# RWKV-6 attention followed by a token mixer: one exponential per unit, the last batch's values loaded like the rest, zero products in the array's gaps, and another order of steps

## Chip, core and metric

One core of a Trainium2 chip runs the whole kernel: one launch, inputs and output in device memory. The metric is the device time of one execution in microseconds (us). TensorE is called PE, VectorE DVE, ScalarE ACT, GpSimd POOL, and SyncE, which issues nearly all DMAs, SP.

## The reference

```python
for t in range(S):        # B, H, S, D = 4, 8, 768, 48
    cur = einsum('bhd,bhe->bhde', u * k[t], v[t])
    y[t] = einsum('bhd,bhde->bhe', r[t], state + cur)
    state = w[t][:, :, :, None] * state + einsum('bhd,bhe->bhde', k[t], v[t])
x = y.transpose(0, 2, 1, 3).reshape(B, S, H * D)          # 4 x 768 x 384
W = (x @ w_q) @ (x @ w_k).T / sqrt(64)                    # per batch
out = relu(W @ x) @ w_out
```

## The kernel before

A **unit** is 256 time steps of one batch, in two chunks (c = 0, 1) of 128; there are 12 units (n = 0 to 11), three to a batch. A partition holds two neighbouring steps (j = 0, 1) of each of the 8 heads, so a load (`load`, L231) moves 1024 pieces of 384 bytes for each of w, k, r and v. Per unit:

- `ln` (ACT, L409) takes the logarithm of w; `cw` (PE, L431) multiplies it with a triangular matrix CM, which gives cumulated sums in PSUM; `ep` and `en` (ACT, L447 and L455) take exp of plus and minus that. `ep` is two instructions, one for each j, because positions inside a chunk are laid out in four interleaved groups of 32 (the permutation matrix PM).
- `k16`, `r16`, `v16` cast to bf16; `kT`, `rT` (PE, L468) transpose k and r through PM; `ks` copies k out of PSUM; `qT` = r k; `RT` = r ep (DVE); `KT` = k en (POOL, or DVE).
- `vp` (PE, L549) brings v into the same order of positions, and `VB` copies it out of PSUM. For the last batch (`WHOLE`) there is no `v16` and no `vp`: four DMAs (`vw`, L244), one to each group of 32 partitions, bring the batch's values already in order, in pieces of 192 bytes, and `VB` casts from there.
- `A` (PE) = KT times RT per head and chunk; `AM` (DVE, L597) masks it, 24 times 1024 columns; `kb` and `kd` transpose and scale KT; `sn` and `SB` (PE, DVE L660) carry the state from chunk to chunk; `ya` and `yi` (PE) sum the output; `dps`, `dd`, `Vd` make the term of u; `X` (DVE, L712) adds both.
- `xt`, `XT`, `qk`, `QK` give the mixer's two projections. After a batch's last unit `T` and `TS` form one matrix for the batch, and per unit `mx`, `rl`, `fp`, `os`, `st` make the output: product, relu, product, copy, store.

The program is not written in this order. Each piece is a step, and three tables written out by hand set everything: `ORDER` (L82) is the order in which all steps are emitted, and so each engine's in-order queue, SP's of DMAs included; `WAYS` (L124) picks the engine of each step that can run on several; `BANKS` (L129) gives each PSUM buffer its bank. A step waits for its inputs and for the release of its buffer. Most buffers come in rings: four each for the loaded w, k, r, v and for the output (`os`), two for the rest. The steps `z` (L859) are fillers: one product of zeros with 512 columns into a PSUM bank, read by nobody; `WARM` = 12 of them stand in ORDER. Nine more such products open the program (L253).

Of the kernel before, what the change touches and what calls it, by code (L numbers as in the profile page):

```python
# [32 lines left out]
class Plan:  # L33
# [89 lines left out]
]  # L123
WAYS = (  # L124
    "PDDPDADDPDPAAPPAAccEADPPDdAAAPEDEcEAADPAdPAAPEDEEAAAAAAAAAAPDPPAAPEAcEEDDAPDdPDDPEAEEEDA"
    "PPDPPADPeAcEDAAAAAAAAPPAPPADPEAEcEAAPADPPADPEAEceDDPPDPPAAPeAceAAAADAADDPPDPPAPEAcEeAAPP"
    "DPPAPeAccEADPPDdPPAPPAEEADAEAAAADADAAAAAAADA"
)
BANKS = [  # L129
# [9 lines left out]
WARM = 12  # L139
# [3 lines left out]
def kernel(  # L143
# [14 lines left out]
    C = 128  # L158
# [12 lines left out]
    LONG = ()  # L171
    WHOLE = (B - 1,)
# [14 lines left out]
    def const(shape, dtype, name):  # L187
# [3 lines left out]
    EW = 136  # L191
# [5 lines left out]
        wg=(4, HW, F32), rg=(4, HW, F32), kg=(4, HW, F32), vg=(4, HW, F32), os=(4, 2 * DM, F32),  # L197
# [22 lines left out]
    PM = const([C, C], BF16, "PM")  # L220
# [15 lines left out]
    def load_long(b, i, tl, ap):  # L236
        for g in range(2):
            o = view(tl, 0, [[2 * D2, NP], [1, 2 * D2]], p0=g, pn=C - 1)
            o = dataclasses.replace(o, ap=[[2 * o.ap[0][0], 64]] + list(o.ap[1:]))
            nc.sync.dma_start(  # L240
                out=o,
                in_=ap[b, ds(g * NP, NP), ds(i * U, U)].rearrange("h (p s) d -> p h (s d)", s=4))

    def load_whole(b, q, tl):  # L244
        nc.sync.dma_start(
            out=view(tl, 0, [[D, H * NCH], [1, D]], p0=64 * (q % 2) + 32 * (q // 2), pn=32),
            in_=dataclasses.replace(v, offset=(b * H * S + q) * D,
                                    ap=[[4 * D, 32], [C * D, H * NCH], [1, D]]))

    def setup():  # L250
# [9 lines left out]
        for q in range(4):  # L260
            rows = ds(64 * (q % 2) + 32 * (q // 2), 32)
            nc.gpsimd.iota(pos0[rows, :], pattern=[[0, 1]], base=q, channel_multiplier=4)
            nc.gpsimd.iota(pos1[rows, :], pattern=[[0, 1]], base=q + 1, channel_multiplier=4)
# [3 lines left out]
        for c in range(2):  # L267
            for j in range(2):
                m = view(CM, j * C, [[64, 2], [32, 2], [1, 32]], p0=c * 64, pn=64)
                nc.gpsimd.affine_select(m, m, pattern=[[1, 2], [2, 2], [4, 32]],  # L270
                                        compare_op=ALU.is_ge, fill=0.0, base=-j,
                                        channel_multiplier=-2)
# [3 lines left out]
        nc.vector.memset(PM, 0.0)  # L276
        m = view(PM, 0, [[64, 2], [32, 2], [1, 32]])
        nc.gpsimd.affine_select(m, m, pattern=[[64, 2], [1, 2], [2, 32]],
                                compare_op=ALU.not_equal, fill=1.0, base=0,
                                channel_multiplier=-1)  # L280
# [5 lines left out]
        for q in range(4):  # L286
            m = view(US, 0, [[64, 2], [32, 2], [1, 32]], p0=64 * (q % 2) + 32 * (q // 2), pn=32)
            nc.gpsimd.affine_select(m, m, pattern=[[1, 2], [2, 2], [4, 32]],
                                    compare_op=ALU.is_gt, fill=0.0, base=-q,
                                    channel_multiplier=-4)  # L290
        for x in (tiles["lw"][1], tiles["k16"][1], tiles["r16"][1]):
            nc.vector.memset(view(x, D, pads), 0.0)
        nc.vector.tensor_scalar_mul(IDU, ID16, UNIT)
        nc.vector.tensor_scalar_mul(gk, gv, UNIT)
        nc.vector.tensor_scalar_mul(US, US, gv)

    def pads(e, x):
# [15 lines left out]
    def wide():  # L313
        return Buf("w")
# [581 lines left out]
```

## Time and profile before

| what | value |
|---|---|
| median of 3 runs | 104.68 us (104.49 to 104.9) |
| the profiled execution | 105.49 us, of which its span 103.8 us |
| instructions | 4460 |
| DMA | 24.68 MB in 56405 packets, mean 238 GB/s |
| loads | w, k, r: 12 each; v: 9, and vw: 4 |
| DVE, ACT, POOL steps | 125, 122, 55 |

The profile is of one execution. Its busy times count an engine from an instruction's start to its end, so neighbouring instructions of one engine overlap by some 0.07 us; where the cost in a row matters, the distance from start to start is used. Matmuls are pipelined with modelled ends, so a busy PE is not an array at its peak. PEclk is the clock granted to the array, 1.00 being the full one. A name such as AM(2,1) is the step AM of unit 2, chunk 1.

### The profile page before, as it was taken

How to read it: one execution, taken by the hardware profiler on the slowest of the kernel's cores; microseconds unless marked ns; L12 is line 12 of the kernel's file. 1: busy time of each engine (PE TensorE's matmuls, PEld its weight loads, DVE VectorE, ACT ScalarE, POOL GpSimd, SP SyncE). 2: the span in 40 equal slices, each digit the busy share in tenths (PEclk: the TensorE clock that was granted, in tenths of full speed). 3: DMA queues.
4: the chain of work that ended last, by engine and by line, in shares of the span. 5: the costliest groups of instructions: out<-in, count | busy, mean ns of one | idle time of the engine just before them, and what ended most of it. 6: DMA issues, size and time to landing. Idle time of an engine off the chain costs nothing.

```text
span 103.8 us, 4460 instructions
## 1 busy us (share of the span) xinstructions
PE 90.4 (87%) x1897; PEld 66.8 (64%) x1899; DVE 85.6 (82%) x155; ACT 81.4 (78%) x138; POOL 64.6 (62%) x78
## 2 busy tenths in 40 slices
PE   5997686999998999999998999979998999999800
PEld 2344564867876887677776877768677687867400
DVE  6295996897889999999999999999999899856020
ACT  6368787875899798899997999898988894938710
POOL 6808507576069979795798969989996456000000
PEclk9999995555579999999999999999999999999995
DMA  1999999989979999999999999998990087007691
GB/s 35 319 323 325 324 258 279 309 214 290 315 201 237 350 325 259 292 327 263 245 303 242 265 304 236 170 174 174 246 348 20 6 317 295 3 6 283 253 334 43
DMA packets 56405, 24.68 MB, mean 238 GB/s; under 512 B 54080, under 2 KB 55232, under 8 KB 56384
## 3 DMA queue, kind: packets, MB, share of 16 engines
q1 hardware_dynamic: 56224, 24.19, 84.9%
q8 instruction: 15, 0.25, 1.0%
q10 hardware_dynamic: 160, 0.20, 0.5%
q14 instruction: 6, 0.05, 0.1%
HBM read 19.66 MB, written 4.72 MB: 235 GB/s over the span
## 4 chain that ended last, share of the span: by engine, by line
PE 48%; DVE 17%; DMA 10%; ACT 9%; SPq 7%; issue 4%; DVEq 0%; ACTq 0%
PE PS L179 48%; SPq L232 7%; DMA wg<-in_w_dram 6%; DMA out_dram<-os 4%; DVE X L712 4%; DVE AM L597 3%; DVE qT L508 3%; DVE RT L518 2%; DVE ks L335 2%; ACT os L329 2%; ACT MX L341 2%; ACT lw L409 2%; ACT kd L331 1%; DVE SB L660 1%; ACT en L456 1%
## 5 line engine op out<-in xcount | busy, mean ns | idle before, releaser
L597 DVE TENSOR_TENSOR AM<-PS,US 128x1024 bf16<-128x1024 f32 x24 | 28.8, 1215 | 1.0 <-ACT lw L409 0.9
L528 POOL TENSOR_TENSOR KT<-ks,en 128x1024 bf16<-128x1024 bf16 (+1 forms) x9 | 17.2, 1914 | 12.1 <-PE PS L179 4.3
L577 POOL TENSOR_TENSOR Vd<-VB,dd 128x768 bf16<-128x768 bf16 (+1 forms) x14 | 18.4, 1317 | 3.2 <-ACT dd L329 1.9
L179 PEld LDWEIGHTS <-KT 48*128 48x128 bf16 (+1 forms) x300 | 10.8, 98 | 6.3 <-issue 4.0
L449 ACT ACTIVATE ep<-PS 128x512 bf16<-128x512 f32 (+1 forms) x28 | 13.6, 550 | 1.3 <-PE PS L179 1.2
L456 ACT ACTIVATE en<-PS 128x1024 bf16<-128x1024 f32 (+1 forms) x14 | 12.7, 912 | 2.2 <-PE PS L179 1.8
L179 PE MATMUL PS<-wo,MX 128*128 128x384 bf16 x72 | 13.4, 326 | 0.0
L712 DVE SCALAR_TENSOR_TENSOR X<-PS,gx,Vd 128x384 bf16<-128x384 f32 x22 | 12.5, 610 | 1.0 <-PE PS L179 0.7
L179 PE MATMUL PS<-RT,KT 48*128 48x128 bf16 x192 | 10.2, 228 | 1.7 <-POOL KT L528 0.4
L423 POOL CAST r<-rg 128x768 bf16<-128x768 f32 x10 | 8.4, 844 | 4.0 <-DMA rg<-in_r_dram 4.0
L409 ACT ACTIVATE lw<-wg 128x768 bf16<-128x768 f32 x12 | 10.2, 852 | 0.7 <-DMA wg<-in_w_dram 0.7
L331 ACT ACTIVATE kd<-PS,gk 128x768 bf16<-128x768 bf16 (+1 forms) x11 | 8.4, 762 | 1.4 <-PE PS L179 1.4
L341 ACT ACTIVATE MX<-PS 128x768 bf16<-128x768 f32 (+1 forms) x13 | 8.7, 688 | 0.7 <-PE PS L179 0.5
L179 PE MATMUL PS<-Z 128*128 128x512 bf16 x19 | 7.5, 522 | 1.8 <-DVE Z L252 1.2
L179 PEld LDWEIGHTS <-MX 128*128 128x128 bf16 x72 | 6.5, 98 | 3.9 <-issue 0.3
L518 DVE TENSOR_TENSOR RT<-PS,ep 128x1024 bf16<-128x1024 bf16 (+1 forms) x14 | 8.4, 605 | 0.8 <-ACT ep L449 0.8
L179 PE MATMUL PS<-VB,AM 128*128 128x48 bf16 x192 | 8.8, 189 | 0.0
L329 ACT COPY os<-PS 128x768 f32<-128x768 f32 (+1 forms) x11 | 7.3, 693 | 1.8 <-DMA out_dram<-os 1.0
L179 PE MATMUL PS<-CM,lw 64*128 64x128 bf16 x192 | 8.3, 232 | 0.4
L329 ACT COPY XT<-PS 128x768 bf16<-128x768 bf16 (+1 forms) x9 | 6.5, 732 | 2.5 <-PE PS L179 2.3
L508 DVE TENSOR_TENSOR qT<-PS,ks 128x1024 bf16<-128x1024 bf16 x12 | 8.2, 683 | 0.0
L179 PEld LDWEIGHTS <-lw 64*128 64x128 bf16 x192 | 6.3, 101 | 1.8 <-ACT lw L409 1.0
(90 smaller groups left out, 196.1 us busy)
## 6 DMA issues: line engine op xcount, KB each, us to landing
kg<-in_k_dram SPq DMA_DIRECT2D x12, 384.0 KB, 5.4
wg<-in_w_dram SPq DMA_DIRECT2D x12, 384.0 KB, 5.1
rg<-in_r_dram SPq DMA_DIRECT2D x12, 384.0 KB, 5.5
vg<-in_v_dram SPq DMA_DIRECT2D x9, 384.0 KB, 6.0
out_dram<-os SPq DMA_DIRECT2D x9, 384.0 KB, 4.1
vw<-in_v_dram SPq DMA_DIRECT2D x4, 288.0 KB, 6.6
out_dram<-os SPq DMA_DIRECT2D x5, 192.0 KB, 3.2
wof<-in_moe_w_out_dram SPq DMA_DIRECT2D x1, 576.0 KB, 6.4
```

The source lines that it names most:

```text
L179: return nc.tensor.matmul(o, l, rr, start=start, stop=stop, skip_group_check=True, is_transpose=trans)
L329: nc.scalar.copy(o, i)
L341: nc.scalar.activation(o, i, ACT.Relu)
L409: nc.scalar.activation(view(lw.tile, 0, [[64, H], [512, 2], [1, D]]), view(g["wg"].tile, 0, [[D2, H], [D, 2], [1, D]]), ACT.Ln, bias=0.0, ...
L449: nc.scalar.activation(view(ep.tile, cs[0] * NP * EW + off, [[EW, NP * len(cs)], [step, 2], [1, 32]]), view(at(cw), cs[0] * 512 + j * 64, ...
L456: nc.scalar.activation(en.tile[:, ds(cs[0] * 512, w_)], at(cw)[:, ds(cs[0] * 512, w_)], ACT.Exp, bias=0.0, scale=-1.0)
L508: lambda e: nc.vector.tensor_tensor(plain(qT.tile), turned(512), plain(ks.tile), ALU.mult),
L518: nc.vector.tensor_tensor(plain(RT.tile, cs, 32), turned(512, cs, True), plain(ep.tile, cs, EW // 4), ALU.mult)
L528: x.tensor_tensor(KT.tile[:, cols], ks.tile[:, cols], en.tile[:, cols], ALU.mult)
L577: (nc.vector if e == "D" else nc.gpsimd).tensor_tensor(Vd.tile[:, cols], VB.tile[:, cols], view(dd.tile, cs[0] * H, [[1, len(cs) * H], [0, ...
L597: AMs[c] = add(("AM", n, c), "D", lambda e, c=c, A=A: nc.vector.tensor_tensor(view(AM[c].tile, 0, [[C, 8], [1, C]]), view(at(A), 0, [[C, 8 ...
L712: nc.vector.scalar_tensor_tensor(view(X.tile, 2 * i * DM + hh * D, [[D2, H], [1, D]]), view(at(y), hh * 512, [[D, H], [1, D]]), gx, view(V ...
```

## The change

The positions of a chunk go from four groups of 32 to two of 64, PM gives way to the identity ID16, and with that `ep` becomes one instruction. `WHOLE` becomes empty, so the last batch's v is loaded, cast and multiplied like the others. `WARM` goes from 12 to 24. ORDER, WAYS and BANKS are replaced. Two new options (`EXACT`, `KEYS`) come with empty settings and emit nothing; an old one (`LONG`), which was empty, goes.

```diff
-    LONG = ()
-    WHOLE = (B - 1,)
+    EXACT = ()
+    KEYS = ()
+    WHOLE = ()
-WARM = 12
+WARM = 24
-    EW = 136
+    EW = 132
...
-        for q in range(4):
-            rows = ds(64 * (q % 2) + 32 * (q // 2), 32)
-            nc.gpsimd.iota(pos0[rows, :], pattern=[[0, 1]], base=q, channel_multiplier=4)
-            nc.gpsimd.iota(pos1[rows, :], pattern=[[0, 1]], base=q + 1, channel_multiplier=4)
+        for j in range(2):
+            rows = ds(64 * j, 64)
+            nc.gpsimd.iota(pos0[rows, :], pattern=[[0, 1]], base=j, channel_multiplier=2)
+            nc.gpsimd.iota(pos1[rows, :], pattern=[[0, 1]], base=j + 1, channel_multiplier=2)
...
             def f_ep(e, cs=cs, w_=w_):
-                for off, step, j in ((68, 34, 0), (34, -33, 1)):
-                    nc.scalar.activation(
-                        view(ep.tile, cs[0] * NP * EW + off,
-                             [[EW, NP * len(cs)], [step, 2], [1, 32]]),
-                        view(at(cw), cs[0] * 512 + j * 64, [[C, NP * len(cs)], [32, 2], [1, 32]]),
-                        ACT.Exp, bias=0.0, scale=1.0)
+                nc.scalar.activation(
+                    view(ep.tile, cs[0] * NP * EW + 66, [[EW, NP * len(cs)], [-65, 2], [1, 64]]),
+                    at(cw)[:, ds(cs[0] * 512, w_)], ACT.Exp, bias=0.0, scale=1.0)
...
-                               PM[rows, rows], trans=True)
+                               ID16[rows, rows], trans=True)
...
-                    e, view(QK.tile, i * QS, [[64, 6], [2, 32], [1, 2]]),
-                    view(at(qk), 0, [[64, 6], [1, 32], [32, 2]])), [qs], QK, [qk], cols=384)
+                    e, QK.tile[:, ds(i * QS, 384)], at(qk)[:, ds(0, 384)]), [qs], QK, [qk],
+                        cols=384)
```

The new tables, read step by step:

- **SP** starts w(0), k(0), w(1), r(0), k(1), r(1), v(0), v(1), k(2), w(2), r(2), w(3), w(4), k(3), v(2), r(3), k(4) (before: k(0), w(0), r(0), w(1), r(1), k(1), v(0), v(1), w(2), r(2), k(2), w(3), v(2), k(3), weights, r(3), r(4)). The first store stands between the loads of v(9) and v(10); before, all stores stood behind all loads.
- **DVE** (125 to 123 steps): `kd` 2 to 6, `QK` 4 to 1, `dd` 4 to 1, `rl` 2 to 3, `os` 4 to 3 (halves counted), one `VB` less, one `Vd` more, one `pads` less; `KT` stays at 5, of other units.
- **ACT** (122 to 125): `VB` 8 to 12, `QK` 7 to 10, `dd` 8 to 11, `kd` 11 to 7, `k16` 3 to 1.
- **POOL** (55 to 57): `v16` 8 to 11, `k16` 8 to 10, `VB` 3 to 0, `Vd` 14 to 13, `pads` 0 to 1.
- **PE** (232 to 247 steps): three `vp` more and 12 fillers more. Ten fillers stand ahead of A(0,1), six from there to cw(4), eight between mx(1) and xt(8).

More of the change, by code (lines that the diff above doesn't have):

```diff
@@ L82 @@
 ORDER = [
[40 rows of a table removed]
[41 rows of a table added]
 ]
 WAYS = (
-    "PDDPDADDPDPAAPPAAccEADPPDdAAAPEDEcEAADPAdPAAPEDEEAAAAAAAAAAPDPPAAPEAcEEDDAPDdPDDPEAEEEDA"
-    "PPDPPADPeAcEDAAAAAAAAPPAPPADPEAEcEAAPADPPADPEAEceDDPPDPPAAPeAceAAAADAADDPPDPPAPEAcEeAAPP"
-    "DPPAPeAccEADPPDdPPAPPAEEADAEAAAADADAAAAAAADA"
+    "PPDPDDDDPDAAADPAAEceAAPPDPPAAPEAccEAAPPDPPAAPEAcEAAAAAAAAAPPDdPADPEDEcEDAPPADPAAPEDEEEAA"
+    "APDdPAAPeDEeDAADAAAAAPPDPPAAPEDcceAAPPDPPAAPEDccEAAPPAPPAAPeAcEDAAAAAAADPPDPPAAPEAEEEAAP"
+    "ADPPAAPeDEEeADPPDdPPAAPPAEEAADEDADADDDAAAAAAADA"
 )
 BANKS = [
[6 rows of a table removed]
[7 rows of a table added]
 ]
-WARM = 12
+WARM = 24
 @with_exitstack
@@ L196 @@
     RINGS = dict(
-        wg=(4, HW, F32), rg=(4, HW, F32), kg=(4, HW, F32), vg=(4, HW, F32), os=(4, 2 * DM, F32),
+        wg=(4, HW, F32), rg=(4, HW, F32), kg=(4, HW + 16, F32), vg=(4, HW, F32), os=(4, 2 * DM, F32),
         kd=(2, KW, BF16), lw=(2, 1024, BF16), r16=(2, 1024, BF16), k16=(2, 1024, BF16),
@@ L219 @@
     ID16 = const([C, C], BF16, "ID16")
-    PM = const([C, C], BF16, "PM")
+    ID32 = const([C, C], F32, "ID32")
     IDU = const([C, C], BF16, "IDU")
@@ L234, in load @@
             in_=ap[b, :, ds(i * U, U)].rearrange("h (p j) d -> p h (j d)", j=2))
[L236 to L242, printed above, removed]
     def load_whole(b, q, tl):
+        n_ = H // 2 * NCH
+        j, q = q % 2, q // 2
         nc.sync.dma_start(
-            out=view(tl, 0, [[D, H * NCH], [1, D]], p0=64 * (q % 2) + 32 * (q // 2), pn=32),
-            in_=dataclasses.replace(v, offset=(b * H * S + q) * D,
-                                    ap=[[4 * D, 32], [C * D, H * NCH], [1, D]]))
+            out=view(tl, q * n_ * D, [[D, n_], [1, D]], p0=64 * j, pn=64),
+            in_=dataclasses.replace(v, offset=(b * H * S + j) * D + q * n_ * C * D,
+                                    ap=[[D2, 64], [C * D, n_], [1, D]]))
     def setup():
@@ L268, in setup @@
             for j in range(2):
[L269 to L272, printed above, removed]
+                m = view(CM, j * C, [[64, 2], [1, 64]], p0=c * 64, pn=64)
+                nc.gpsimd.affine_select(m, m, pattern=[[1, 2], [2, 64]], compare_op=ALU.is_ge,
+                                        fill=0.0, base=-j, channel_multiplier=-2)
         nc.vector.memset(ID16, 0.0)
@@ L275, in setup @@
                                 base=0, channel_multiplier=-1)
[L276 to L280, printed above, removed]
         for x in (tiles["lw"][0], tiles["k16"][0], tiles["r16"][0]):
@@ L285, in setup @@
         nc.vector.memset(US, 1.0)
[L286 to L290, printed above, removed]
+        for j in range(2):
+            m = view(US, 0, [[64, 2], [1, 64]], p0=j * 64, pn=64)
+            nc.gpsimd.affine_select(m, m, pattern=[[1, 2], [2, 64]], compare_op=ALU.is_gt,
+                                    fill=0.0, base=-j, channel_multiplier=-2)
         for x in (tiles["lw"][1], tiles["k16"][1], tiles["r16"][1]):
@@ L294, in setup @@
         nc.vector.tensor_scalar_mul(gk, gv, UNIT)
+        if EXACT or KEYS:
+            nc.vector.tensor_copy(ID32, ID16)
+        for x in tiles["kg"] if KEYS else ():
+            nc.vector.memset(x[:, ds(HW, 16)], 0.0)
         nc.vector.tensor_scalar_mul(US, US, gv)
@@ L368, in cast @@
                                         view(wq_f, 0, [[DH, NK], [0, 2], [1, DH]]), scale)
-            nc.gpsimd.tensor_copy(view(wk_sb, 0, [[DH, NK], [32, 2], [1, 32]]),
-                                  view(wk_f, 0, [[DH, NK], [1, 2], [2, 32]]))
+            nc.gpsimd.tensor_copy(wk_sb, wk_f)
         wts["qk"] = add(("wcast",), "P", cast, [dma(("wts",), f_qk)])
@@ L390, in unit @@
         fine = each if split else both
-        whole, long = b in WHOLE, n in LONG
+        whole = b in WHOLE
+        exact, keys = n in EXACT and not whole, n in KEYS
         g = {}
         for name, ap in (("wg", w), ("kg", k), ("rg", r)) + (() if whole else (("vg", v),)):
-            f = load_long if name in ("kg", "rg") and long else load
             g[name] = ring(name)
-            g[name + "L"] = dma((name, n), lambda e, ap=ap, f=f, x=g[name].tile: f(b, i, x, ap),
+            g[name + "L"] = dma((name, n), lambda e, ap=ap, x=g[name].tile: load(b, i, x, ap),
                                 buf=g[name])
@@ L418, in f @@
                 op = dict(A=nc.scalar.copy, D=nc.vector.tensor_copy, P=nc.gpsimd.tensor_copy)[e]
-                if long:
-                    op(view(o.tile, 0, [[64, NP], [256, 4], [1, D]]),
-                       view(g[src].tile, 0, [[2 * D2, NP], [D, 4], [1, D]]))
-                else:
-                    op(view(o.tile, 0, [[64, H], [512, 2], [1, D]]),
-                       view(g[src].tile, 0, [[D2, H], [D, 2], [1, D]]))
+                op(view(o.tile, 0, [[64, H], [512, 2], [1, D]]),
+                   view(g[src].tile, 0, [[D2, H], [D, 2], [1, D]]))
             return o, add((name, n), ways, f, [g[src + "L"]], o, [g[src]])
-        k16, k16s = cast16("k16", "kg", "PAD")
+        if not keys:
+            k16, k16s = cast16("k16", "kg", "PAD")
         r16, r16s = cast16("r16", "rg", "PAD")
@@ L466, in unit @@
         kr = wide()
+        kf = wide() if keys else kr
         def transposed(name, src, step, place):
@@ L470, in f @@
                 o = at(kr, BF16)
-                if long:
-                    for hp in range(2):
-                        for s in range(4):
-                            for c in range(2):
-                                rows = ds(c * 64, 64)
-                                x = c * 1024 + place + hp * C + (s % 2) * 64 + (s // 2) * 32
-                                mm(view(o, x, [[256, 2], [1, 32]]),
-                                   src.tile[rows, ds(s * 256 + hp * 128, 128)],
-                                   PM[rows, rows], trans=True)
-                    return
                 for hp in range(NP):
@@ L486, in f, with f_kf @@
                                src.tile[rows, ds(j * 512 + hp * 128, 128)],
-                               PM[rows, rows], trans=True)
+                               ID16[rows, rows], trans=True)
             return add((name, n), "E", f, [step], kr, [src], mode=1)
+        def f_kf(e):
+            for hp in range(NP):
+                for j in range(2):
+                    for c in range(2):
+                        rows = ds(c * 64, 64)
+                        mm(at(kf)[:, ds(c * 512 + hp * C + j * 64, 64)],
+                           view(g["kg"].tile, 2 * hp * D2 + j * D, [[D2, 2], [1, 64]], 64 * c, 64),
+                           ID32[rows, rows], trans=True)
         def turned(place, cs=(0, 1), runs=False):
-            return view(at(kr, BF16), place + cs[0] * 1024, [[1024, len(cs)]] * (len(cs) > 1) +
-                        ([[32, 16], [1, 32]] if runs else [[1, 512]]))
+            x = [[64, 8], [1, 64]] if runs else [[1, 512]]
+            if keys and place == 0:
+                return view(at(kf), cs[0] * 512, [[512, len(cs)]] * (len(cs) > 1) + x)
+            return view(at(kr, BF16), place + cs[0] * 1024, [[1024, len(cs)]] * (len(cs) > 1) + x)
         def plain(t, cs=(0, 1), run=0):
-            y = 16 * (run or 32)
+            y = 8 * (run or 64)
             return view(t, cs[0] * y, [[y, len(cs)]] * (len(cs) > 1) +
-                        ([[run, 16], [1, 32]] if run else [[1, y]]))
-        kTs = transposed("kT", k16, k16s, 0)
+                        ([[run, 8], [1, 64]] if run else [[1, y]]))
+        if keys:
+            kTs = add(("kT", n), "E", f_kf, [g["kgL"]], kf, [g["kg"]], mode=1, cols=4)
+        else:
+            kTs = transposed("kT", k16, k16s, 0)
         rTs = transposed("rT", r16, r16s, 512)
         ks = ring("ks")
-        kss = add(("ks", n), "AD", lambda e: copy(e, plain(ks.tile), turned(0)), [kTs], ks, [kr],
-                  cols=1024)
+        kss = add(("ks", n), "AD", lambda e: copy(e, plain(ks.tile), turned(0)), [kTs], ks, [kf],
+                  cols=4 if keys else 2)
         qT = ring("qT")
@@ L517, in f_RT @@
             def f_RT(e, cs=cs):
-                nc.vector.tensor_tensor(plain(RT.tile, cs, 32), turned(512, cs, True),
-                                        plain(ep.tile, cs, EW // 4), ALU.mult)
+                nc.vector.tensor_tensor(plain(RT.tile, cs, 64), turned(512, cs, True),
+                                        plain(ep.tile, cs, EW // 2), ALU.mult)
             def f_KT(e, cs=cs):
@@ L532, in unit @@
                     cols=512 * len(cs), half=half,
-                    more=dict(P=([kss], [ks]), D=([kss], [ks]), d=([kTs], [kr])))
+                    more=dict(P=([kss], [ks]), D=([kss], [ks]), d=([kTs], [kf])))
             for c in cs:
@@ L543, in unit @@
         else:
-            v16, vp = ring("v16"), wide()
-            v16s = add(("v16", n), "PAD", lambda e: copy(
-                e, view(v16.tile, 0, [[D, H], [DM, 2], [1, D]]),
-                view(g["vg"].tile, 0, [[D2, H], [D, 2], [1, D]])), [g["vgL"]], v16, [g["vg"]])
+            v16, vp = None if exact else ring("v16"), wide()
+            if not exact:
+                v16s = add(("v16", n), "PAD", lambda e: copy(
+                    e, view(v16.tile, 0, [[D, H], [DM, 2], [1, D]]),
+                    view(g["vg"].tile, 0, [[D2, H], [D, 2], [1, D]])), [g["vgL"]], v16, [g["vg"]])
             def f_vp(e):
@@ L553, in f_vp @@
                         rows = ds(c * 64, 64)
-                        mm(x[ds(j * 64, 64), ds(c * 512, DM)], PM[rows, rows],
-                           v16.tile[rows, ds(j * DM, DM)])
-            vps = add(("vp", n), "E", f_vp, [v16s], vp, [v16], mode=3)
+                        if exact:
+                            mm(x[ds(j * 64, 64), ds(c * 512, DM)], ID32[rows, rows],
+                               view(g["vg"].tile, j * D, [[D2, H], [1, D]], 64 * c, 64))
+                        else:
+                            mm(x[ds(j * 64, 64), ds(c * 512, DM)], ID16[rows, rows],
+                               v16.tile[rows, ds(j * DM, DM)])
+            vps = add(("vp", n), "E", f_vp, [g["vgL"] if exact else v16s], vp,
+                      [g["vg"] if exact else v16], mode=3, cols=4 if exact else 1)
             VBs = add(("VB", n), "AD", lambda e: copy(
@@ L661, in unit @@
                     view(SB.tile, 0, [[D, NP], [1, D]]), view(at(sn), 0, [[D, NP], [1, D]]),
-                    view(ep.tile, c * NP * EW + 32, [[EW, NP], [0, D]]), ALU.mult),
+                    view(ep.tile, c * NP * EW + 64, [[EW, NP], [0, D]]), ALU.mult),
                 [sns, eps[c]], SB, [sn, ep])
@@ L778, in unit @@
                 batch["k"].append(add(("wkc", n, c0), "AD", lambda e, c0=c0, qk=qk: copy(
-                    e, view(QK.tile, i * QS + U + c0 * DH, [[2, 32], [1, 2]]),
-                    view(at(qk), 0, [[1, 32], [32, 2]])), [q1], QK,
+                    e, QK.tile[:, ds(i * QS + U + c0 * DH, DH)], at(qk)[:, ds(0, DH)]), [q1], QK,
                     [qk], cols=DH))
                 batch["q"].append(add(("wqc", n, c0), "AD", lambda e, c0=c0, wq=wq: copy(
-                    e, view(QK.tile, i * QS + c0 * C, [[64, 2], [2, 32], [1, 2]]),
-                    view(at(wq), 0, [[64, 2], [1, 32], [32, 2]])), [q2], QK,
+                    e, QK.tile[:, ds(i * QS + c0 * C, C)], at(wq)[:, ds(0, C)]), [q2], QK,
                     [wq], cols=C))
```

94 rows, old and new, of tables (BANKS, ORDER) are left out of this document.

## The prediction

> **What bounds the kernel.** First the page: busy shares, then its slices of 2.6 us.
>
> ```profile
> PE 90.4 (87%) x1897; PEld 66.8 (64%) x1899; DVE 85.6 (82%) x155; ACT 81.4 (78%) x138; POOL 64.6 (62%) x78
> ...
> DVE  6295996897889999999999999999999899856020
> ...
> PEclk9999995555579999999999999999999999999995
> ```
>
> DVE is full from slice 13 to 33 and has holes before and after; the clock is down in slices 7 to 12. The windows view says how much:
>
> ```profile
> 10.00:15.00 5.00, 3.74 (x108) 2.85 (x109) 5.00 (x10) 3.76 (x7) 1.86 (x3) 1.00 1.12 302
> 15.00:20.00 5.00, 4.01 (x80) 2.97 (x77) 3.68 (x6) 4.08 (x7) 2.72 (x3) 0.60 1.08 289
> 20.00:25.00 5.00, 4.80 (x87) 3.78 (x87) 4.71 (x9) 2.61 (x4) 4.36 (x5) 0.50 0.94 245
> 25.00:30.00 5.00, 4.63 (x108) 3.94 (x103) 3.55 (x6) 4.56 (x9) 0.69 (x2) 0.53 1.07 286
> 30.00:35.00 5.00, 4.54 (x121) 3.65 (x117) 4.91 (x8) 4.33 (x7) 5.00 (x5) 1.00 0.94 248
> ...
> 65.00:70.00 5.00, 4.29 (x125) 3.51 (x124) 4.88 (x8) 4.76 (x8) 4.51 (x5) 1.00 1.13 176
> ```
>
> Columns: PE, PEld, DVE, ACT, POOL busy, granted clock, DMA share, GB/s. From 15 to 30, DVE idles 3.06 us (15.00 less 3.68, 4.71, 3.55); from 30 to 90 the same view adds up to 1.9 of 60. So the kernel has three stages. To 30 us it waits for landings and for an array at half clock; to 89.8 (end of X(11,1)) DVE sets the pace; then comes a tail of 13 us. In the first, DVE's timeline shows what is late:
>
> ```profile
> 16.06 0.35 DVE L660 TENSOR_TENSOR SB<-PS,ep 128x192 bf16<-128x192 f32 x1
> 17.38 0.87 DVE L423 CAST k<-kg 128x768 bf16<-128x768 f32 x1 [0.97 <-DMA kg<-in_k_dram]
> ...
> 20.16 0.69 DVE L523 TENSOR_TENSOR KT<-PS,en 128x1024 bf16<-128x1024 bf16 x1 [0.51 <-PE PS L179]
> 26.24 1.23 DVE L597 TENSOR_TENSOR AM<-PS,US 128x1024 bf16<-128x1024 f32 x1 [0.89 <-ACT lw L409]
> ```
>
> The clock falls at 16.04 and returns at 29.70 (a window of 1 us at 16 shows 0.52, one at 29 shows 0.65), after the least busy of these windows:
>
> ```profile
> 5.80:9.21 3.41, 2.55 (x53) 1.29 (x52) 2.53 (x7) 2.55 (x8) 1.10 (x1) 1.00 1.17 324
> 9.21:12.63 3.42, 2.71 (x83) 2.02 (x83) 3.10 (x7) 2.45 (x5) 2.65 (x4) 1.00 1.17 326
> 12.63:16.04 3.41, 2.44 (x48) 1.77 (x46) 3.41 (x6) 3.04 (x7) 0.00 (x0) 1.00 1.04 272
> ```
>
> 13.66 us is four times 3.41. The array was 2.55 and 2.71 us busy ahead of windows at full clock, 2.44 ahead of the fall.
>
> **The first stage.** I lay out the new queues by hand with the durations of before. Loads land 1.36 us apart, by rank: the first at 4.1 (k16(0) starts at 4.15), the ninth at 15.0, k(2) as eleventh at 17.35, k(3) as fourteenth at 22.5.
>
> - w(0) has rank 1, not 2: ln(0) starts at 4.15, not 5.35. w(1) has rank 3, not 4. With ln 0.75, cw 0.6, the halves of ep and en 0.53 each and whole ones 0.9, ep(1) is done at 10.7 (before: 12.95).
> - k16(0) now costs DVE 0.8, while it waits anyway. AM(0,0) starts at 11.0 (10.87), behind r(0), now rank 4; but ks(1), 0.6, is already done.
> - New holes: 0.7 ahead of UB (r(0) lands at 7.8); 0.9 ahead of X(0), whose Vd(0,1) stands on POOL behind v16(1) and k16(2), which waits for k(2) (rank 9, 15.0); 0.45 ahead of SB(1,0), as kd(1) and VB(1) stand on ACT behind ln(2), which waits for w(2) (rank 10, 16.2); 0.2 ahead of ks(2). In all 2.3, against 4.2 in before (0.8 and 0.3 to 9.9, then 3.06).
> - Work in this stretch: without KT(1), KT(2), kd(1), kd(2) (-0.6, -0.6, -0.53, -0.34) and k16(2) (-0.8); with ks(2), KT(3), kd(3) (+0.6, +0.6, +0.53) and Vd(0,0) (no such row on DVE; between dd, 0.16, and the 512-wide KT, 0.47; I take 0.4, nearest in size): -0.74.
>
> The point where AM(2,0), RT(3), qT(3) are done is 32.4 in before. 4.2 - 2.3 + 0.74 = 2.6: 29.8, **2.6 us earlier** (followed instruction by instruction, the same layout gives 29.3; the difference of 0.5 is kept for the range). This holds at full clock. Six fillers stand between A(0,1) and cw(4), where one stood; each has 0.38 us of busy time, and 0.11 more would have lifted the window that fell to the level of one that did not. I take it that the clock holds.
>
> **The second stage.** DVE up to X(11,1), rows less their 0.07 overlap: kd four more, +2.1; rl(3) +0.87; Vd +0.4; KT +0.1; QK three fewer, -1.37; VB -0.87; XT -0.47; dd -0.25: +0.5, of which +0.06 lies in the first stage (-0.74 there, but k16(2)'s 0.8 only moved ahead of it). So **+0.45** after it. That pads(1), 0.7, runs among the waits at 6 us is in the walk.
>
> - One exponential:
>
> ```profile
> L449 ACT ACTIVATE ep<-PS 128x512 bf16<-128x512 f32 x20 | 11.0, 606 | 0.9 <-PE PS L179 0.8
> L456 ACT ACTIVATE en<-PS 128x1024 bf16<-128x1024 f32 x10 | 10.3, 1030 | 1.4 <-PE PS L179 1.0 <-DVE k L423 0.2 <-issue 0.2
> ```
>
> A pair costs 1.10 busy (start to start 0.98), one `en` 1.03 (0.89): 0.09 by ten units and 0.04 by four halves, 1.1 us. The write with step -65 starts at an odd column, as half of the old ones did; bounds 0 and 1.1, I take 0.9. ACT otherwise: VB +2.9, QK +1.2, os and XT +1.0, kd -3.3, k16 -1.5, small ones -0.4. ACT ends 1.0 lower, beside DVE: **0**; from nothing to -0.5 where RT waits for ep.
> - Last batch: POOL casts v16 (0.83) in place of VB (0.83), **0**. PE gets three vp of 0.29 from start to start, ACT three VB; between 30 and 90 the windows leave PE 2.9 idle and ACT 6.2, so beside DVE **0**. If that cover is gone, 0.9.
> - Its DMAs: while vw runs, the windows show 157 to 208 GB/s at full share (row 65:70), 313 before that. 1.18 MB takes 6.9 us there, at 313 GB/s 3.8. After k16(3) at 22.5 no engine waits for a landing of w, k, r or v, so **0** by itself; but k(11), w(11), r(11) stood behind vw and left SP at 67.5 to 71.2 (landing 5 us later, ln(11) at 77.86). With DVE 2 us earlier, they would be near late; without vw they are not. SP's stores: st(0) waits for os(0), long done; st(3), which waits for os(3), stands behind all loads.
> - Fillers: 0.22 from start to start. Ten in the opening replace others' waits. Eight later are 1.8 us of PE against its idle 2.9; each takes a bank, so it can wait for a reader. Bounds 0 and 1.8; I take **+0.3**, nearer to nothing as DVE is the fuller engine.
>
> **The tail.** X(11,1) to xt, XT, wk, wkc, T, mx, fp, os, stores; fp(6) stands ahead of wk(11) in both. The chain of waits:
>
> ```profile
> 93.47 0.81 ACT os L329
> 94.28 0.02 issue
> 94.30 4.61 DMA out_dram<-os
> 98.91 0.03 issue
> 98.94 0.05 DVEq L335
> 98.98 0.04 issue
> 99.03 0.56 DVE os L335
> ```
>
> os(11) waits for the store of os(7), as the ring has four; six stores fill the last 9 us. os(6) moves from DVE to ACT behind rl(8): 0.95 becomes 0.80, and the wait is as long. **0**, within 0.4.
>
> **Sum.** -2.6 + 0.45 + 0.3 = -1.85 on the profiled execution: span 103.8 to 101.95, with the 1.7 outside it 103.6 for 105.49. The median of before is 0.8 below that execution; taken from it, 104.68 - 1.85 = **102.8 us**.
>
> **Rivals.**
>
> 1. **The clock falls again.** In my layout PE waits near 17.7 for kd(1), and the window from 16.04 to 19.45 holds some 2.2 us, less than the 2.44 that preceded the fall. Then 19.45 to 29.7 is at half clock, 10.2 of 13.66 us. Of DVE's holes there, 3.06 less the 0.97 of a landing, this share is 2.1 x 10.2 / 13.66 = 1.6: 102.8 + 1.6 = 104.4. A rule of the Trainium skill speaks for it: TensorE: Matmul & The Clock Gate, Part 4, says that transposes do not count as activity like other products. Without them (kT, rT, kb, uT) the timeline's groups give 1.96, 2.06 and 2.2 us for the three windows above, the most ahead of the fall: here the trace does not agree. The same page (Terms) prices a slow clock at its time by one half, 6.8 us, an estimate from its rule; by that a held clock would bring the sum to -6.4 (-6.8 + 0.45), but the rows have only 3.06 of DVE's idle time to win.
> 2. **The array becomes the bound: slower.** Between mx(1) and xt(8) PE has eight fillers more and then vp: 1.8 + 0.9 = 2.7, nearly all of its idle 2.9 between 30 and 90. If that idle time is not where they stand (a filler waits for its bank and holds the queue), DVE loses all of it; with the clock down as well, 104.4 + 2.7 - 0.3 = 106.8. It decides once PE is late for more than one unit in a row. For: the chain is 48% PE. Against: DVE and not PE is full.
> 3. **The lead is given back**: new holes of 2 us in the middle (before has 1.9, little for any order), 104.8.
>
> **Chances.** Forecast 0.42, the clock 0.20, the array 0.25, given back 0.13. What a measurement of this kernel can tell from no change is about 0.5%, 0.5 us. The clock's case lies near its edge, so half of it counts as faster and half as the same; of the last, half as the same and half as slower: faster 0.52, same 0.16, slower 0.32. The range runs from the forecast less 1.7 (tail 0.4, ep 0.5, fillers 0.3, the layout 0.5), 101.1, to 106.6, just short of the array's case at its worst.
>
> **What would show it.** The clock row: 1.00 from 16 to 30. AM(2,0), RT(3), qT(3) done near 29.8. DVE without more than 2 us of holes from 30 to X(11,1), which ends near 88. No landing of w, k, r or v waited for after 30 us, 300 GB/s where vw was. A tail of 13 us. I am wrong if X(11,1) ends after 90, or if PE waits little and DVE much between 30 and 85.

## The result and the profile after

| compared on one chip | before, median us | changed, median us | ratio, 95% interval |
|---|---|---|---|
| first comparison | 104.74 | 103.18 (102.97 to 103.29) | 0.9851 [0.9824, 0.9877] |
| `r_after` | 104.94 | 103.51 (103.2 to 104.69) | 0.9890 [0.9833, 0.9948] |
| `r_after_b` | 106.16 | 104.23 (103.52 to 107.14) | 0.9793 [0.9745, 0.9841] |

The first comparison is the result: 1.56 us faster, where 1.85 was forecast. The two others are the same kernel again, on other chips, with the experiments below; their ratios differ by 1%, so differences under 1% between comparisons are not read here. The medians are of all executions; the ratios leave out those more than 1.5% above the fastest of the same kernel.

The profiled execution took 103.12 us, span 101.4. Its page, DVE and the granted clock in slices of 2.5 us:

```profile
DVE  6677599999999999998999999999999997927400
...
PEclk9998599999999999999999999999999999999999
```

DVE is full from slice 6 on, seven slices earlier than before, and the clock is down in one stretch, earlier and shorter. The windows view of the changed kernel (PE, PEld, DVE, ACT, POOL busy, clock, DMA share, GB/s):

```profile
15.00:20.00 5.00, 3.54 (x98) 3.16 (x98) 4.92 (x8) 3.79 (x6) 4.62 (x6) 1.00 0.93 248
20.00:25.00 5.00, 4.35 (x140) 3.54 (x138) 5.00 (x10) 4.34 (x6) 4.08 (x4) 1.00 1.08 293
25.00:30.00 5.00, 4.48 (x111) 3.41 (x114) 5.00 (x8) 3.76 (x6) 3.82 (x5) 1.00 0.99 254
...
65.00:70.00 5.00, 4.93 (x161) 4.20 (x155) 5.00 (x11) 4.98 (x8) 5.00 (x5) 1.00 0.97 277
```

DVE's 3.06 us of idle time between 15 and 30 are 0.08 now, and 277 GB/s stand where vw ran at 176. The whole difference, in two stretches: to the point where AM(2,0), RT(3) and qT(3) are done, and from there to the end of X(11,1). First the changed kernel, then the kernel before:

```profile
0.00:31.08 31.08, 24.70 (x499) 16.28 (x506) 26.73 (x54) 21.11 (x32) 21.97 (x35) 0.95 1.01 270
31.08:87.94 56.86, 55.56 (x1360) 42.67 (x1362) 55.37 (x91) 51.97 (x81) 43.41 (x40) 1.00 0.87 245
```

```profile
0.00:32.40 32.40, 27.05 (x478) 18.49 (x480) 25.14 (x57) 23.56 (x39) 18.09 (x37) 0.79 0.99 264
32.40:89.82 57.42, 54.90 (x1352) 42.97 (x1353) 55.48 (x93) 51.19 (x84) 46.54 (x42) 1.00 0.90 240
```

The third column of busy times is DVE. Its idle time to X(11,1) falls from 7.26 + 1.94 = 9.20 us to 4.35 + 1.49 = 5.84, 3.36 less; its busy time rises from 80.62 to 82.10, 1.48 more. The sum is -1.88, and X(11,1) ends at 87.94 instead of 89.82. The first stretch gives 1.32 of this (idle time 2.91 less, work 1.59 more), the second 0.56. With a tail of 13.46 for 13.98 this is the span's 2.4. By the profiled executions the gain is 2.37 us, by the medians 1.56, as the execution of before that was profiled lay 0.75 above its median.

### The profile page after: what moved, and what is told of

The parts are those of the page before. It is cut to its first block, busy times and chain, and to the rows that moved or that the text cites. A ratio compares the mean times of both kernels' runs of the same rounds, so it can differ in the third digit from the quotient of the medians.

```text
span 101.4 us, 4504 instructions
## 1 busy us (share of the span) xinstructions
PE 88.8 (88%) x1921; PEld 64.3 (63%) x1930; DVE 86.4 (85%) x151; ACT 80.0 (79%) x127; POOL 65.4 (64%) x74
## 4 chain that ended last, share of the span: by engine, by line
PE 44%; DVE 25%; ACT 9%; DMA 7%; issue 6%; POOL 3%; SPq 1%; DVEq 0%; ACTq 0%; POOLq 0%
PE PS L182 44%; DVE AM L595 8%; DMA wof<-in_moe_w_out_dram 7%; DVE X L710 5%; DVE ks L329 3%; ACT ep L438 2%; ACT en L443 2%; DVE RT L510 2%; ACT VB L323 2%; DVE SB L658 1%; POOL Vd L575 1%; DVE r L412 1%; ACT lw L402 1%; DVE qT L500 1%; POOL wo L329 1%
## 5 line engine op out<-in xcount | busy, mean ns | idle before, releaser
L575 POOL TENSOR_TENSOR Vd<-VB,dd 128x768 bf16<-128x768 bf16 (+1 forms) x13 | 17.2, 1330 | 8.3 <-ACT dd L323 4.9
L182 PEld LDWEIGHTS <-KT 48*128 48x128 bf16 (+1 forms) x300 | 10.2, 96 | 5.2 <-issue 3.5
L438 ACT ACTIVATE ep<-PS 128x1024 bf16<-128x1024 f32 (+1 forms) x14 | 12.8, 921 | 0.6 <-PE PS L182 0.6
L402 ACT ACTIVATE lw<-wg 128x768 bf16<-128x768 f32 x12 | 10.2, 858 | 1.9 <-DMA wg<-in_w_dram 1.9
L182 PE MATMUL PS<-Z 128*128 128x512 bf16 x24 | 10.1, 506 | 1.5 <-DVE Z L249 1.2
L323 ACT CAST VB<-PS 128x768 bf16<-128x768 f32 x12 | 9.7, 811 | 1.0 <-PE PS L182 0.9
L323 ACT COPY os<-PS 128x768 f32<-128x768 f32 (+1 forms) x12 | 8.4, 702 | 2.6 <-PE PS L182 2.4
L182 PE MATMUL PS<-CM,lw 64*128 64x128 bf16 x192 | 7.8, 224 | 2.2 <-ACT lw L402 1.2
L329 POOL CAST v<-vg 128x768 bf16<-128x768 f32 x11 | 9.0, 829 | 0.1
L335 ACT ACTIVATE MX<-PS 128x768 bf16<-128x768 f32 (+1 forms) x12 | 8.1, 708 | 1.2 <-PE PS L182 1.1
L412 POOL CAST k<-kg 128x768 bf16<-128x768 f32 x10 | 8.3, 826 | 0.3 <-DMA kg<-in_k_dram 0.3
```

Source lines behind the costliest of these rows:

```text
L182: return nc.tensor.matmul(o, l, rr, start=start, stop=stop, skip_group_check=True, is_transpose=trans)
L323: nc.scalar.copy(o, i)
L329: x.tensor_copy(o, i)
L402: nc.scalar.activation(view(lw.tile, 0, [[64, H], [512, 2], [1, D]]), view(g["wg"].tile, 0, [[D2, H], [D, 2], [1, D]]), ACT.Ln, bias=0.0, ...
L412: op(view(o.tile, 0, [[64, H], [512, 2], [1, D]]), view(g[src].tile, 0, [[D2, H], [D, 2], [1, D]]))
L438: nc.scalar.activation(view(ep.tile, cs[0] * NP * EW + 66, [[EW, NP * len(cs)], [-65, 2], [1, 64]]), at(cw)[:, ds(cs[0] * 512, w_)], ACT.E ...
```

## The experiments

My theory was the prediction's: the new order, with fillers that hold the clock, takes idle time from DVE's first 30 us, and all else is worth nothing. Its rivals: the clock alone does it; the fillers cost as much as they give; the other edits matter.

### Without the fillers

```diff
-            if s["fn"] is not None:
+            if s["fn"] is not None and s["key"] not in DROP:
```

`DROP` is a new list; here it names the 24 z.

> The changed kernel without its 24 filler products (the nine that open the program stay). If the held clock is what was won (the prediction's account), the array falls to half clock for 10 us or more of the first 30 and DVE's holes come back: 104.2 to 105.0 us. If the new order of loads and engines won it, the clock being worth some 0.13 us per window of 3.41 us (the four runs of the changed kernel so far: 102.97 us at a mean clock of 0.999, 103.12 at 0.983, 103.24 at 0.969, 103.29 at 0.971), then four or five slow windows give at most 103.8, less what the fillers themselves cost.

Measured: 103.64 us, ratio 0.9854 [0.9795, 0.9913]. Its windows:

```profile
10.00:15.00 5.00, 3.85 (x81) 2.70 (x81) 4.66 (x9) 2.81 (x6) 3.90 (x4) 0.50 1.17 323
15.00:20.00 5.00, 5.00 (x115) 4.24 (x115) 4.84 (x8) 3.39 (x6) 3.23 (x5) 0.67 0.93 243
```

The clock was at half for 10.24 us, 7.9 to 18.1, yet DVE was 4.66 and 4.84 of 5 busy. In the new order the fillers are not needed for the gain, and neither is a full clock in these 10 us.

Only the eight late ones out (z 23, 5, 1, 6, 10, 20, 18, 22 in `DROP`):

> The changed kernel without the eight fillers between mx(1) and xt(8); the other sixteen stay. If DVE sets the pace there, nothing is to be had: 102.9 to 103.2 us. If the array does (the prediction's second rival), 8 x 0.22 = 1.8 us less: 101.4.

Measured: 103.46 us, 0.9834 [0.9781, 0.9888], no different. They cost nothing that shows: the array is not the bound where they stand. This run and `e1_no_fillers` were timed in one comparison, and the mean clock of its trace is 0.99 for 0.94 there; the two ratios differ by 0.2%, less than either interval allows to tell.

### Six fillers more in the old order

The kernel before with `WARM` = 18; in ORDER (not shown) two of the new z stand behind kb(1), four behind dps(1).

```diff
-WARM = 12
+WARM = 18
```

> The kernel before with six fillers more: two behind kb(1), four behind dps(1), in waits of the array near 14 and 16 us. If the clock alone is worth DVE's holes in the first stage, it stays up from 16 to 30 us and the time falls by 1.6 us to 103.1. If a slow window costs some 0.13 us, four of them give 0.5: 104.2 us. If the clock falls all the same, 104.7.

Measured: 103.98 us, 0.9789 [0.9717, 0.9860]: by the ratio as much as the whole change. The eight executions lie far apart, from 102.11 to 105.86; by the medians (103.98 for 105.26) the gain is 1.3 us. Its windows:

```profile
15.00:20.00 5.00, 3.97 (x92) 2.63 (x87) 4.12 (x6) 3.74 (x7) 2.72 (x3) 1.00 1.02 268
20.00:25.00 5.00, 3.92 (x98) 2.94 (x97) 4.87 (x9) 3.56 (x6) 3.89 (x5) 1.00 0.90 227
25.00:30.00 5.00, 4.59 (x98) 3.87 (x96) 4.57 (x9) 3.96 (x7) 2.48 (x2) 0.67 0.95 251
```

The clock holds to 26, and DVE idles 1.44 us from 15 to 30 instead of 3.06. So in the old order the clock did cost time, some 1.3 us in this trace: of the 1.62 us less, 0.27 is a shorter wait for k(2)'s landing, and AM(2,0) is done at 31.08 instead of 32.40. This profiled execution took 105.86 us, the longest of the eight, and shows what came late in it. Its DVE timeline:

```profile
82.67 0.69 DVE L334 COPY ks<-PS 128x1024 bf16<-128x1024 bf16 x1 [1.99 <-PE PS L178]
```

ks(11) waits 2 us for unit 11's transposes on PE, and rT(11) among them for r(11), which landed 2.44 us after POOL stood ready for it: SP had issued the four vw from 63.15 to 69.95, then k(11) at 70.06 and r(11) at 72.85. That is the case which the prediction called near late.

### The new code in the old order

ORDER, WAYS, BANKS (not shown) and `WARM` = 12 of before in the changed code, `WHOLE` = (B - 1,). Row order, single `ep`, the `kg` tiles (16 columns wider in the changed code) and a new form of the vw loads (64 partitions each instead of 32) remain.

```diff
-WARM = 24
+WARM = 12
...
-    WHOLE = ()
+    WHOLE = (B - 1,)
```

> The new layout and the single exponential with the tables of before (order, engines, banks), its 12 fillers and the vw loads of the last batch (now four of 64 partitions each, still in pieces of 192 bytes). If ACT is not on the path, one exponential is worth nothing: 0.995 to 1.000 of the kernel before. If it is, 1.0 us: 0.99. If the whole gain lies in layout and exponential and not in the order, 0.985.

Measured: 106.29 us, 1.0113 [1.0067, 1.0160], slower. One candidate was the single exponential: it can't start until SB has read the whole ep tile, while the first of the two could. ep(2) on ACT in this kernel, and in the same kernel with two exponentials:

```profile
20.19 1.04 ACT L434 ACTIVATE ep<-PS 128x1024 bf16<-128x1024 f32 x1 [0.85 <-DVE SB L654]
```

```profile
19.77 1.12 ACT L435 ACTIVATE ep<-PS 128x512 bf16<-128x512 f32 x2
```

```diff
-                nc.scalar.activation(
-                    view(ep.tile, cs[0] * NP * EW + 66, [[EW, NP * len(cs)], [-65, 2], [1, 64]]),
-                    at(cw)[:, ds(cs[0] * 512, w_)], ACT.Exp, bias=0.0, scale=1.0)
+                for j, off in ((0, 66), (1, 1)):
+                    nc.scalar.activation(
+                        view(ep.tile, cs[0] * NP * EW + off, [[EW, NP * len(cs)], [1, 64]]),
+                        view(at(cw), cs[0] * 512 + j * 64, [[C, NP * len(cs)], [1, 64]]),
+                        ACT.Exp, bias=0.0, scale=1.0)
```

> The changed code with the old step order, banks and fillers, and vw for the last batch, but the ep exponential in two instructions again; with the single one this kernel stood at 1.0113 [1.0067, 1.016]. Theory A, the single instruction has to wait for the whole of the ep buffer and for the whole of cw where the first half used to start early: 0.998 to 1.004, and SB's wait ahead of ep(2) at 20.2 us is gone from its first half. Theory B, the loads are slower with the new vw shape or the wider kg tiles: still 1.008 to 1.016, and the landings 0.45 us later than in the kernel before from 10 us on. Either way the new row order alone costs nothing.

Measured: 1.0004 [0.9970, 1.0038] (105.98 for 106.16). The ratio is the one that theory A named, but the trace does not bear it out: the wait is gone, and X(11,1) starts at 89.61 instead of 89.79, only 0.2 us earlier; X(1) starts no earlier (29.89, 29.82). Most of the 0.9 us between the two spans lies in the tail, where the last `os` on DVE starts at 98.33 instead of 99.63. Theory B's sign is in both traces: k16(2), which waits for k(2), starts at 17.81 (one exponential) and 17.88 (two) for 17.38 in the kernel before, and X(11,1) at 89.79 and 89.61 for 89.20. The two ratios come from different comparisons and lie 1.1% apart, hardly more than those of one and the same kernel. The same edit in the changed kernel, alone and with four fillers moved:

> The changed kernel with ep as two instructions again, one for each j, in the new layout (two runs of 64 columns). ACT gets some 1.0 us more (0.09 in ten units, 0.04 in four halves). Beside a full DVE this costs 0 to 0.3: 103.2 to 103.5 us. If ACT's queue is on the path in all units, 104.2.

Measured: 102.83 us, 0.9764 [0.9704, 0.9824].

> The changed kernel with two exponentials and with its four fillers between uT and kT(1) moved (z15 and z17 ahead of cw(1), z12 and z2 ahead of rT(0)). Theory A, the single instruction costs: 0.973 to 0.980, some 0.9 us under the changed kernel of this call. Theory B, it costs nothing and the earlier 0.9764 was the chip's spread: 0.983 to 0.989, as the changed kernel.

Measured: 104.79 us, 0.9895 [0.9846, 0.9944], beside 0.9793 [0.9745, 0.9841] for the changed kernel in the same comparison, 1% slower. One points below the changed kernel, the other above it, so neither is read: what the single exponential costs or gains in the new order is not told from its spread. Theory A found no support there; what made the 1.0113 stays open. Moving the four fillers alone (z15, z17 ahead of cw(1); z12, z2 ahead of rT(0)):

> The changed kernel with four of its opening fillers moved forward: two from ahead of kT(1) to ahead of cw(1), two to ahead of rT(0), where the array waits 0.9 us each in the profile. If they delay kT(1) and ks(1) where they stand (DVE idles 1.1 us there in the profile), and keep the clock up better where they go, DVE gains 0.5 to 1 us: 0.975 to 0.98 of the kernel before. If the landings behind set the pace anyway, as the changed kernel.

Measured: 103.40 us, 0.9835 [0.9788, 0.9882] beside 0.9890: the intervals overlap. In its trace no hole stands ahead of ks(1), and AM(0,0) starts at 12.52 for 13.49.

### The last batch

The changed kernel with vw in the places of vg(9) to vg(11). In a first version VB(11) stood ahead of the last readers of VB(9), whose tile it takes, so that unit 9 read other values; its time (1.0150) answers nothing:

> The changed kernel with the last batch's values in the old way: four loads vw in the places of v(9) to v(11), VB cast on POOL in the places of v16, no vp. If vw is hidden, the same as the changed kernel. If it holds up the loads behind it (w, k, r of unit 11), which the earlier DVE now needs sooner, waits for landings near 75 us show, and 0.5 to 2 us are lost: 0.99 to 1.005 of the kernel before.

In the second, VB(9) and VB(10) stand on POOL where v16(9) and v16(10) stood, and VB(11) behind ya(9).

```diff
-    WHOLE = ()
+    WHOLE = (B - 1,)
```

> The changed kernel with only the values of the last batch taken back: four vw loads of 288 KB at the places of vg(9), vg(10) and vg(11), VB(9) to VB(11) on POOL, no vp(9) to vp(11). Theory A, vw's 192-byte packets hold up k, w and r of unit 11 once DVE is two us early (the case that the prediction called near late): 0.993 to 1.003, DVE waits of 0.5 us and more behind a landing between 75 and 88 us, and under 200 GB/s at 60 to 72 us. Theory B, the transfer is hidden: within 0.003 of the changed kernel of this call, at most 0.2 us of such waits.

Measured: 107.39 us, 0.9998 [0.9945, 1.0052], beside 0.9793: with vw, the whole gain is gone. The twelve executions lie from 105.10 to 112.52, and their median is above the 106.16 of the kernel before. The expected place was not the one that showed. ACT, DVE and POOL, in the profiled execution (107.49 us, near that median):

```profile
70.18 0.83 ACT L410 CAST r<-rg 128x768 bf16<-128x768 f32 x1 [2.56 <-DMA rg<-in_r_dram]
...
71.78 0.69 DVE L327 COPY ks<-PS 128x1024 bf16<-128x1024 bf16 x1 [2.47 <-PE PS L180]
...
77.07 0.82 POOL L327 CAST VB<-vw 128x768 bf16<-128x768 f32 x1 [5.90 <-DMA vw<-in_v_dram]
```

DVE's longest hole after 60 us is the one ahead of ks(10): r(10), issued at 63.24, just ahead of the first vw, lands 2.56 us late, ACT stands for it, and rT(10) on PE behind ACT. In `r_after_b`, where single loads follow, r(10) was issued at 63.40, and no engine waits for its landing. From 70.5 to 77.4 the array is then at half clock (0.51 in this window). VB(9) needs all four vw, as each holds a part of every unit; POOL stands for 5.9 us, KT(10) behind it too, but here no long hole of DVE ends by it; in the first version's trace, with VB(9) in the same place, one of 2.99 us ahead of SB(9,0) does. Unit 11's loads are late as well (r(11) issued at 75.58; in `r_after_b` at 72.85). The run doesn't part these, and the order was laid out for single loads, so 2% is what vw costs in this order, not in the best order for it.

### The changed kernel again

> The changed kernel itself, beside the other three on one chip: 0.985 of the kernel before. It is here as their reference.

The profiled execution took 104.69 us with the clock at 1.00 throughout (span 103.0). From its windows:

```profile
40.00:50.00 10.00, 8.37 (x204) 6.12 (x204) 8.39 (x15) 7.99 (x13) 7.28 (x7) 1.00 0.91 231
```

In the 103.12 us execution this row has 257 GB/s and 9.65 us of DVE. From 30 to 60 DVE idles 3.08 us here, 0.60 there; w, r and v land late up to 2.0 us each, six of such waits over 0.5 us after 30. DVE's longest hole there, 1.59 us ahead of the qT at 48.86, comes behind such a wait: POOL's cast of r had stood 1.53 us for its load. In this execution landings held DVE back where they did not in the other.

> The changed kernel once more, as the measure for the three beside it. Ratio to the kernel before 0.985 to 0.989, as in its two earlier comparisons.

## Why the prediction was right, and where not

- **The sum** was -1.85; the medians gave -1.56, the two profiled executions -2.37. Sign and main source are right: the gain is idle time of DVE ahead of 30 us. That the size came so near is luck: the first stage gave -1.32 where -2.6 was forecast, the second -0.56 where +0.75 was, the tail -0.52 where 0 was. The first two errors, 1.28 and 1.31, cancel, and so X(11,1) ended at 87.94, "near 88".
- **The first stage's terms were off.** "4.2 - 2.3 + 0.74" had the idle time fall by 1.9 and the work by 0.74; the idle time of this stretch fell by 2.91, and the work rose by 1.59. AM(0,0) starts at 13.49, not 11.0, and AM(2,0), RT(3), qT(3) are done at 31.08, not 29.8. Three DVE instructions were mis-sized, each beside a POOL instruction: Vd(0,0) took 1.21 (0.4 taken), r16(0) 1.51 (0.49 before), and US 1.36 (0.39 before; now beside a memset of `kd` on POOL, 3.90 to 5.07). That is 2.8 us together, where the work came out 2.33 above the forecast. DVE's timeline of the changed kernel, then POOL's:

```profile
3.79 1.36 DVE L289 TENSOR_SCALAR US<-US,gv 128x128 f32<-128x128 f32 x1 [0.29 <-POOL US L279]
...
8.03 1.51 DVE L412 CAST r<-rg 128x768 bf16<-128x768 f32 x1
...
17.39 1.21 DVE L575 TENSOR_TENSOR Vd<-VB,dd 128x384 bf16<-128x384 bf16 x1
```

```profile
7.74 1.39 POOL L520 TENSOR_TENSOR KT<-ks,en 128x512 bf16<-128x512 bf16 x1 [2.24 <-DVE ks L329]
...
17.36 0.83 POOL L575 TENSOR_TENSOR Vd<-VB,dd 128x384 bf16<-128x384 bf16 x1
```

  r16(0) and Vd(0,0) end 0.41 us after POOL's, as if they had run only then: 9.54 for 9.13, 18.60 for 18.19. In the nine other traces of the new order they end 0.41 or 0.42 after POOL's too and last from 0.95 to 1.51; beside Vd(0,0) that is not always the same instruction (in `r_after` it is k16(2)). With POOL idle beside it, US takes 0.29 (`e5_new_code_old_order`, at 3.78). The Trainium skill has this rule (SBUF — State Buffer, Terms): DVE and GpSimd take turns at a pair of ports, held for a whole instruction. These ends agree with it; no run was made to test it.
- **The holes**: ahead of UB 0.82 (0.7 expected). Those expected ahead of X(0), SB(1,0) and ks(2), 1.55 in sum, are not there. The one ahead of ks(1) was not expected at all. DVE, then PE, of the changed kernel:

```profile
12.89 0.69 DVE L329 COPY ks<-PS 128x1024 bf16<-128x1024 bf16 x1 [1.10 <-PE PS L182]
```

```profile
12.24 0.60 PE L182 MATMUL PS<-ID,k 64*128 64x64 bf16 x16
```

  k16(1) was done at 10.25; kT(1) stood behind uT, four fillers and kb(0) at half clock; "ten in the opening replace others' waits" was wrong for these four. Out of the way (`e8_fillers_moved`), they gain nothing that can be told.
- **The clock** was held from 16 to 30 as forecast, but fell at 9.33, which I had not looked for:

```profile
5.92:9.33 3.41, 1.87 (x40) 0.96 (x36) 3.05 (x6) 3.10 (x6) 1.39 (x1) 1.00 1.18 318
9.33:12.74 3.41, 2.92 (x46) 1.65 (x49) 1.64 (x5) 1.54 (x2) 1.65 (x2) 0.52 1.17 325
...
16.16:19.57 3.41, 2.57 (x70) 2.33 (x69) 3.41 (x4) 2.79 (x5) 3.12 (x4) 1.00 0.91 242
```

  It fell after a window of 1.87 us busy and returned after one. Rival 1 priced 10.2 us of half clock at 1.6 us. In the new order, e1's 10.24 us cost nothing to be told (0.9854 for e2's 0.9834), as DVE was supplied anyway; in the old order, e4's fillers won back about that sum (1.3 by the medians, 2.2 by the ratio). The rival's price was about right for the old order and wrong for the one it was meant for. A rule of the Trainium skill prices slow clock at half its time (TensorE: Matmul & The Clock Gate, Part 1, HAM oscillation): 5.1 us for e1, an estimate; e1 lies 0.2 us from e2, each known to some 0.6 us. The prediction's test of the rule on transposes misread its rows: without kT, rT, kb and uT, PE's timeline of before gives 1.97, 1.89 and 1.89 us for the three windows, not 1.96, 2.06 and 2.2. The window ahead of the fall is not the most, so the trace speaks neither for that rule nor against it.
- **The second stage** was to lose 0.45 + 0.3. It lost nothing: 56.86 us from the same point to X(11,1) for 57.42, DVE's idle time 1.49 for 1.94. The late fillers were 0 (`e2_no_late_fillers`), the lower end of "bounds 0 and 1.8".
- **One exponential, 0**: right as far as can be told; ACT's ep takes 12.8 us for 13.6.
- **The last batch, 0 "by itself"**: not tested, as no run has single loads in the old order. With DVE two us earlier, the single loads count: with vw in this order, `e6b_new_with_vw` loses the whole lead.
- **The tail** was to be 0 within 0.4; it is 0.52 shorter. The end of the chain of waits of the changed kernel:

```profile
86.84 9.16 PE PS L182 x86
96.03 0.48 ACT os L323
```

  No store stands in it, where one of 4.61 us had stood ahead of os(11).
- **No landing waited for after 30 us** holds for the 103.12 us execution, not for every one (`r_after`), which is rival 3, the lead given back, in one execution. Rival 2, the array, is out.

**What stays open**: why the new code was slower in the old order in one comparison; how much of `e6b_new_with_vw`'s loss is r(10)'s late landing, how much the half clock behind it, how much VB's place; whether the changed kernel and the old order with six fillers differ. No kernel tried was shown to beat the changed one: `e3_two_exps` and `e4_before_more_fillers` stood lowest, within the spread of its own three comparisons (0.9793 to 0.9890) or just below it.

## What to carry to other kernels

Ask of a slow clock, first, whether the engine that sets the pace waits for the array while it is slow; six zero products in the old order answer that for nothing, and here they gave 1.3 us by the medians, not much less than a new order. An edit that the old order's trace prices at nothing (the last batch's loads) can decide whether a lead is kept in the new one, so price each edit in the order that it is to stand in. Add up a forecast by stage and compare it by stage: a sum can come out right by errors that cancel. And take an instruction's length from a row with the same neighbour on POOL.

## What the runs showed of the hardware

- The modelled busy time of the array does not order the clock's windows: it returned after 2.92 us busy of 3.41 at half clock in the changed kernel (9.33 to 12.74), while before it stayed down after 3.22 and 3.05 (19.45 to 26.28).
- A DVE instruction that read and wrote SBUF beside a POOL instruction ended 0.41 or 0.42 us after POOL's, for r16(0) and Vd(0,0) in ten traces. qT and RT, which read PSUM, took the same 0.68 us beside POOL's KT (14.63 to 15.90 in the changed kernel) as with POOL idle (13.20 to 14.48 in the kernel before).
- With no fall of the clock at all (`r_after`), one execution of the same program was still 1.5 us longer than another of the same comparison (104.69, 103.20), with 231 GB/s in the stretch where the 103.12 us execution had 257.
